# Separate places for the q copies of two head pairs, and a written TensorE order at the start

## The chip, the cores and the metric

The kernel runs on one core of one Trainium2 chip. The metric is the device time of one execution in microseconds; the figure is the median over several runs. Times on a trace are microseconds from the start of the span.

## The reference

The reference chains three stages over 8 sequences of 576 tokens and 512 features (8 heads of 64).

```
scores = (q @ k^T) / sqrt(64), masked in blocks of 64 (row block >= column block)
attn   = exp(scores - max); attn /= sum + 1e-9;  x = attn @ v          # attention
gate   = sigmoid(causal convolution of x with 5 taps per feature)
x      = (gate * (x @ w_val)) @ w_out                                  # gated convolution
u      = x + real(fft over tokens and features of x)                   # Fourier mixing
un     = (u - mean) / sqrt(var + 1e-6)
out    = u + relu(un @ w_ch1) @ w_ch2                                  # feed-forward layer
```

All of it is float32. The kernel holds it by splitting each operand of a matmul into a high part and a low rest (hi + lo) and adding two or three products.

## The kernel before, in words

The program has two phases. `phase2` is the feed-forward layer; it is not touched. `phase1` does attention, gated convolution and Fourier mixing, batch by batch. The change lies in its first part.

Attention goes by head pairs: two heads of one sequence share the 128 partitions, 64 rows each. There are 32 pairs, four to a sequence, and each is cut into nine units (NB = 9): units 0 to 7 are the four query blocks of 128 rows for either head, unit 8 holds the last 64 rows of both heads. The main loop (L973) runs over units n = 9 * p + i and issues, for each n, work of several ages: the score matmuls of unit n (`emit_qk`), row maxima (`emit_max`) and exponentials (`emit_exp`) of a unit or two before, the transposes of the probabilities of unit n - 6 (`emit_t`), and, at two places of the first five pairs, the product with v (`emit_near`). Behind every fourth pair a dense stage for that sequence (`dense`: psv, psx, psy and pss matmuls) is appended and taken in small steps beside later units. How many steps a unit takes is set by a credit: RATE0 = 0.9 a unit up to n = N0 = 60, RATE = 1.25 after it. The preparation of weights (`prep_weights`: loads into XA, decoding on ScalarE and VectorE, folds on POOL, then the DFT tables into `dft_t`) moves along with the steps.

Before its scores, q and k of a pair are loaded by SP (`load`, L346 and L348) into two raw buffers, and `split` makes high and low parts: `k_hi` (L57 by `copy`), `k_dup` (four SP copies, L385), `k_lo` (POOL, L380), `q_hi` (ScalarE, L366) and `q_lo` (VectorE, L369) into QHL, and `q_last` (two SP copies into QD, L374), which feeds unit 8. `spread(p, g)` then sends QHL on to the tiles QQ[h][g] that the score matmuls read (L427, L428): for either head one SP copy of the high part (L398) and one of the low part (L400), so four for each half g. Half g = 0 feeds units 0 to 3, half g = 1 units 4 to 7. QHL and QQ exist once. So q of pair p + 1 may be split only when the copies of pair p have gone out, and a half of QQ may be overwritten only when the score matmuls of pair p that read it are done: split(p + 1) is issued in unit 0 of pair p, its two halves are spread in units 4 and 8.

The stages of `split` form a `Chain`: `tick` runs one stage of each open chain, twice in a unit.

A planner orders the instructions of each engine ahead of time: of those whose inputs it believes ready, the one that was issued first in the program goes first. An engine then runs in that fixed order, and waits on semaphores where an input is late.

Of the kernel before, what the change touches and what calls it, by code (L numbers as in the profile page):

```python
# [17 lines left out]
def kernel(  # L18
# [14 lines left out]
    B, NP, P, S = q.shape  # L33
# [73 lines left out]
    def k_places():  # L107
        return [kp.tile([P, S], F32R, tag=t, name=t) for t in ("K0", "K1", "KP", "KL")]
# [4 lines left out]
    def w_places(f, t):  # L113
        WQ[f] = [x[:, 0:D] for x in t]
# [12 lines left out]
    def phase1():  # L127
        with ExitStack() as c1:
# [14 lines left out]
            QHL = pa.tile([P, 2, S], F32R, name="QHL")  # L143

            QD = [pa.tile([P, 2, P], F32R, name=f"QD{i}") for i in range(2)]

            QQ = [[pa.tile([P, 2, 256], F32R, name=f"QQ{h}{g}") for g in range(2)] for h in range(2)]
# [18 lines left out]
            GH = [pool.tile([P, 2 * N2], F32R, name=f"GH{c}") for c in range(4)]  # L166
# [6 lines left out]
            dft_t = pool.tile([P, dft.shape[1]], F32R, name="dft")  # L173
# [162 lines left out]

            NPAIR = B * NP
            qraw, kraw, KK, KP, KL, VV = {}, {}, {}, {}, {}, {}
            rs = [slice(0, 64), slice(64, 128)]

            def load(p):
# [16 lines left out]
            def split(p):  # L358
                if p >= NPAIR:
                    return  # L360

                *KK[p], KP[p], KL[p] = k_places()
                kk, kh, kl = KK[p], KP[p], KL[p]

                def q_hi():
                    nc.scalar.activation(out=QHL[:, 0, :], in_=qraw[p], func=AF.Copy, scale=0.125)  # L366

                def q_lo():
                    nc.vector.scalar_tensor_tensor(out=QHL[:, 1, :], in0=qraw[p], scalar=0.125,  # L369
                                                   in1=QHL[:, 0, :].bitcast(F32), op0=ALU.mult, op1=ALU.subtract)  # L370

                def q_last():
                    for r in rs:
                        nc.sync.dma_start(out=QD[p % 2][r, :, r].bitcast(F32), in_=QHL[r, :, D:S].bitcast(F32))  # L374

                def k_hi():
                    copy(0, kh, kraw[p])

                def k_lo():
                    nc.gpsimd.tensor_tensor(out=kl, in0=kraw[p], in1=kh.bitcast(F32), op=ALU.subtract)  # L380

                def k_dup():
                    for h in range(2):
                        for r in rs:
                            nc.sync.dma_start(out=kk[h][r, :].bitcast(F32), in_=kh[rs[h], :].bitcast(F32))  # L385

                def both(*f):
                    return lambda: [g() for g in f]

                return Chain(k_hi, both(k_dup, k_lo), wait, q_hi, q_lo, q_last)  # L390

            def spread(p, g):

                if p >= NPAIR:
                    return
                c = slice(256 * g, 256 * g + 256)
                for h in range(2):
                    nc.sync.dma_start(out=QQ[h][g][rs[h], :, :].bitcast(F32),  # L398
                                      in_=QHL[rs[h], 0:1, c].bitcast(F32).to_broadcast([64, 2, 256]))
                    nc.sync.dma_start(out=QQ[h][g][rs[1 - h], 0, :].bitcast(F32), in_=QHL[rs[h], 1, c].bitcast(F32))  # L400
# [12 lines left out]
            def emit_qk(n):  # L413
                p, i = divmod(n, NB)
                if i in (1, 3):

                    return
                if i < 8:

                    L = P * (i // 2 + 1)  # L420
                    w = max(256, L)
                    m = slice(P * (i // 2 % 2), P * (i // 2 % 2) + P)
                    t = sc_tile(n)
                    for u in range(2 if i < 4 else 1):
                        h, o = (u, w * u) if i < 4 else (i % 2, 0)
                        q = QQ[h][i // 4]
                        nc.tensor.matmul(t[:, o:o + w], q[:, 0, m], KK[p][h][:, 0:w], start=True, stop=False)  # L427
                        nc.tensor.matmul(t[:, o:o + w], q[:, 1, m], KL[p][:, 0:w], start=False, stop=True)  # L428
                        scs[n + u] = [(t[:, o:o + L], 0, L)]
                    if i < 4:  # L430
                        twos[n] = t.rearrange("p (h w) -> p h w", h=2)[:, :, 0:L]
                    return

                sc = []
                for k0, w in ((0, 320), (320, 256)):
                    t = sc_tile(n)
                    mm3(t[:, 0:w], QD[p % 2][:, 0], QD[p % 2][:, 1], KP[p][:, k0:k0 + w], KL[p][:, k0:k0 + w], True, True)
                    sc.append((t[:, 0:w], k0, w))
                scs[n] = sc
# [470 lines left out]
            NU = NPAIR * NB  # L910
            LT = 6
# [8 lines left out]
            LA = 1  # L920
# [2 lines left out]
            PN = 5  # L923
            EW = 4
            EX = 3
            N0 = 60
            RATE0 = 0.9
            RATE = 1.25
            N1 = 30
# [11 lines left out]
            prepared = [0]  # L941
            load(0)
            nc.gpsimd.memset(PB[8][:, S:640], 0.0)
            for t in QD + [QQ[h][g][rs[1 - h], 1, :] for h in range(2) for g in range(2)]:
                nc.gpsimd.memset(t.bitcast(F32), 0.0)
            split(0).run()
            spread(0, 0)
            spread(0, 1)
            load_v(0)
            load(1)  # L950
            pend = [prep]
# [1 line left out]
            credit = 0.0  # L953
# [16 lines left out]
                        pend.pop(0)  # L970

            now[0] = 1
            for n in range(NU + LT + LA):  # L973
                if n == N1:
                    now[0] = 0
                p, i = divmod(n, NB)
                credit += RATE if n > N0 else RATE0
                nst = int(credit)
                credit -= nst
                if n < NU:  # L980
                    if i == 6:
                        load(p + 2)
                    if i == 7:
                        load_v(p + 1)
                    if i == 0:
                        split(p + 1)
                    emit_qk(n)
                    if i in (4, 8):
                        spread(p + 1, i // 8)
                    if p == NPAIR - 1 and i in (0, EW):  # L990
                        if i == 0:
                            w_places(0, k_places())
                        for z in range(2):
                            first_weights(2 * (i > 0) + z)
                if n in (NU, NU + EX):

                    if n == NU:
                        w_places(1, k_places())
                    for z in range(2):
                        first_weights(4 + 2 * (n > NU) + z)  # L1000
                old = list(live)
                step(nst // 2)
                tick(old)
                advance(0, n, emit_max, 1)
                advance(1, n, emit_exp)
                pr, ir = divmod(n - FR, NB)
                if n >= FR and PN <= pr < NPAIR and ir == 0:
                    emit_recip(pr)
                old = list(live)
                if 0 <= n - LT < NU:  # L1010
                    emit_t(n - LT)
                advance(0, n, emit_max)
                m = n - LT - LA
                if 0 <= m < NU:
                    pm, im = divmod(m, NB)
                    if pm < PN:
                        if im in (2, 7):
                            emit_recip_near(pm, im // 7)
                        if im == 3:
                            emit_near(pm, 0)  # L1020

                    if im == 8:

                        while pm % NP == 0 and gate_done[0] < pm // NP:
                            step()
                        if pm % NP == 0 and pm:
                            folds[4 * (pm // NP) - 2].run(2)
                        while pm % NP == 1 and pm > NP and val_done[0] < pm // NP:
                            step()
                        if pm < PN:  # L1030
                            emit_near(pm, 1)
                        else:
                            emit_av(pm)
                        if pm % NP == NP - 1:
                            pend.append(dense(pm // NP))
                step(nst - nst // 2)
                tick(old)
                if n >= FR and PN <= pr < NPAIR and ir == 1:
                    emit_factors(pr)
            while pend:  # L1040
                if not drain[0]:
                    drain[0] = 3
                old = list(live)
                step()
                tick(old)
# [611 lines left out]
```

## Time and profile before

| | us |
|---|---|
| median of 3 runs | 1408.18 (1406.77 to 1408.38) |
| the profiled execution, its own time | 1406.78 |
| its span on the trace | 1405.0 |
| TensorE busy in the span | 1349.6 (96%) |
| VectorE (DVE) busy | 1094.1 (78%) |
| ScalarE (ACT) busy | 821.1 (58%) |

Busy times of an engine are the union of its instructions; a busy TensorE is not TensorE at its peak, since the matmuls are pipelined and the granted clock can be lower. An engine's idle time costs nothing where another engine is the bottleneck. Engines in the rows: PE is TensorE, PEld its weight loads, DVE VectorE, ACT ScalarE, POOL GpSimd, SP SyncE, which issues nearly all DMAs (SPq is its queue).

### The profile page before, as it was taken

The numbers are of one execution on the slowest core, as the hardware profiler recorded it, in microseconds if no ns is written. First come the engines' busy times: TensorE is split into PE (matmuls) and PEld (weight loads), VectorE is DVE, ScalarE is ACT, GpSimd is POOL, SyncE is SP. The second block draws the span as 40 slices with busy tenths as digits, with TensorE's granted clock in tenths as the row PEclk, the third lists the DMA queues.
The fourth block names the chain that finished last, engine by engine and source line by source line (L and its number), as shares of the span: only waits on it lengthen the run. The fifth ranks groups of instructions, "written<-read, shape, count | busy, mean of one in ns | idle before, by whom it ended". The sixth has DMA issues, their size and how long they took to land.

```text
span 1405.0 us, 24014 instructions
## 1 busy us (share of the span) xinstructions
PE 1349.6 (96%) x8547; PEld 1186.2 (84%) x8547; DVE 1094.1 (78%) x1965; ACT 821.1 (58%) x1790; POOL 207.7 (15%) x180
## 2 busy tenths in 40 slices
PE   5798999999999999999999999999999999999998
PEld 3576799898989998888777887788888889999998
DVE  5867787887878797989899798599746983796274
ACT  5687777777777777764344244574356534744451
POOL 2423232323232232322100000000000000000000
PEclk9799999999999999999999999999999999999999
DMA  7566566656556565646598996985875479779875
GB/s 211 138 176 189 158 182 154 186 139 176 153 158 158 153 164 155 173 149 236 198 369 290 356 316 211 319 273 195 280 266 201 180 248 328 256 250 319 273 250 188
DMA packets 176755, 308.24 MB, mean 219 GB/s; under 512 B 28270, under 2 KB 106876, under 8 KB 169468
## 3 DMA queue, kind: packets, MB, share of 16 engines
q1 hardware_dynamic: 176096, 306.57, 69.2%
q8 instruction: 68, 1.11, 0.3%
q14 instruction: 51, 0.42, 0.1%
q10 hardware_dynamic: 540, 0.14, 0.1%
HBM read 203.74 MB, written 56.76 MB: 185 GB/s over the span
## 4 chain that ended last, share of the span: by engine, by line
PE 73%; DVE 12%; DMA 5%; ACT 3%; issue 3%; POOL 2%; SPq 2%; DVEq 0%; ACTq 0%; POOLq 0%
PE banks L1421 12%; PE banks L1423 12%; PE banks L1422 12%; PE av L615 4%; PE pt L587 4%; DVE gate L642 2%; PE sc L427 2%; PE o L1518 2%; PE psh L1498 2%; PE psh L1496 2%; PE psh L1497 2%; PE o L1516 2%; PE o L1517 2%; PE sc L428 2%; POOL XA L848 1%
## 5 line engine op out<-in xcount | busy, mean ns | idle before, releaser
L1421 PE MATMUL banks<-o,chunk 128*128 128x512 f32 (+1 forms) x896 | 324.2, 362 | 1.0 <-ACT h L1429 1.0
L1422 PE MATMUL banks<-o,chunk 128*128 128x512 f32 (+1 forms) x896 | 323.9, 362 | 0.0
L1423 PE MATMUL banks<-o,chunk 128*128 128x512 f32 (+1 forms) x896 | 323.9, 362 | 0.0
L473 ACT ACTIVATE PB<-sc,mx 128x128 f32<-128x128 f32 (+4 forms) x320 | 166.5, 525 | 51.0 <-DVE mx L459 27.8
L1421 PEld LDWEIGHTS banks<-o,chunk 128*128 128x128 f32 x896 | 168.2, 188 | 19.1 <-ACT h L1429 1.7
L1423 PEld LDWEIGHTS banks<-o,chunk 128*128 128x128 f32 x896 | 168.2, 188 | 17.6
L1422 PEld LDWEIGHTS banks<-o,chunk 128*128 128x128 f32 x896 | 168.2, 188 | 17.2
L1381 ACT CAST o<-h 128x1024 fp32r<-128x1024 f32 (+1 forms) x112 | 105.4, 944 | 106.9 <-PE banks L1423 86.5
L587 PE MATMUL pt<-ident,PB 128*128 128x128 f32 x800 | 141.9, 283 | 15.1 <-ACT PTb L593 8.2
L1382 DVE TENSOR_TENSOR o<-h,o 128x1024 fp32r<-128x1024 f32 (+1 forms) x112 | 119.7, 1083 | 23.3 <-ACT o L1381 22.9
L587 PEld LDWEIGHTS pt<-ident,PB 128*128 128x128 f32 x800 | 101.0, 144 | 31.9 <-ACT PTb L593 14.5
L642 DVE SCALAR_TENSOR_TENSOR gate<-XF,cw,gate 128x575 f32<-128x575 f32 (+3 forms) x128 | 122.5, 957 | 4.3 <-ACT gate L63 3.6
L459 DVE TENSOR_REDUCE mx<-sc 128x1 f32<-128x384 f32 (+2 forms) x192 | 104.2, 560 | 4.4 <-PE sc L193 2.7
L427 PE MATMUL sc<-K,QQ 128*128 128x256 f32 (+2 forms) x256 | 87.7, 353 | 13.5 <-DMA QQ<-QHL 12.6
L593 ACT COPY PTb<-pt 128x512 f32<-128x512 f32 (+1 forms) x160 | 86.5, 544 | 18.5 <-PE pt L587 17.6
L1429 ACT COPY h<-banks 128x1024 f32<-128x1024 f32 (+1 forms) x64 | 58.0, 906 | 57.3 <-PE banks L1423 57.3
L191 PE MATMUL psx<-GH,we_h 128*128 128x290 f32 x256 | 83.5, 326 | 2.4 <-ACT GH L57 1.5
L191 PE MATMUL psv<-XH,wv_h 128*128 128x288 f32 x256 | 83.5, 327 | 0.4 <-ACT PB L473 0.4
L428 PE MATMUL sc<-KL,QQ 128*128 128x256 f32 (+2 forms) x256 | 82.8, 334 | 0.0
L638 POOL TENSOR_TENSOR XL<-XF,XH 128x576 fp32r<-128x576 f32 x32 | 45.9, 1433 | 249.6 <-ACT XH L57 228.8
L192 PE MATMUL psx<-GL,we_h 128*128 128x290 f32 x256 | 76.2, 298 | 0.5 <-DVE GL L703 0.5
L192 PE MATMUL psv<-XL,wv_h 128*128 128x288 f32 x256 | 76.2, 298 | 0.0
(266 smaller groups left out, 3151.3 us busy)
## 6 DMA issues: line engine op xcount, KB each, us to landing
chunk<-comb_d SPq DMA_DIRECT2D x64, 512.0 KB, 5.0
chunk<-comb_d SPq DMA_DIRECT2D x32, 1024.0 KB, 4.8
chunk<-base_d SPq DMA_DIRECT2D x48, 512.0 KB, 5.9
chunk<-base_d SPq DMA_DIRECT2D x24, 1024.0 KB, 6.3
K<-KP SPq DMA_DIRECT2D x128, 144.0 KB, 2.5
QQ<-QHL SPq DMA_DIRECT2D x128, 128.0 KB, 2.4
rw<-in_w_ch SPq DMA_DIRECT2D x28, 512.0 KB, 8.3
comb_d<-packed SPq DMA_DIRECT2D x12, 1024.0 KB, 10.1
```

The lines of the kernel that those rows point to most:

```text
L191: nc.tensor.matmul(ps, lh, rh, start=first, stop=False)
L192: nc.tensor.matmul(ps, lh, rl, start=False, stop=False)
L427: nc.tensor.matmul(t[:, o:o + w], q[:, 0, m], KK[p][h][:, 0:w], start=True, stop=False)
L428: nc.tensor.matmul(t[:, o:o + w], q[:, 1, m], KL[p][:, 0:w], start=False, stop=True)
L473: nc.scalar.activation(out=PB[i][:, k0:k0 + w], in_=t, func=AF.Exp, bias=nm, accum_out=su[:, at + j:at + j + 1])
L587: nc.tensor.transpose(ps[:, j, :], PB[i][:, (j0 + j) * P:(j0 + j + 1) * P], ident)
L642: nc.vector.scalar_tensor_tensor(out=gate[c][:, s:S], in0=XF[:, 0:S - s], scalar=cw[:, c, 4 - s:5 - s], in1=gate[c][:, s:S], op0=ALU.mult, ...
L1381: nc.scalar.copy(out=o[:, 0], in_=x)
L1382: nc.vector.tensor_tensor(out=o[:, 1], in0=x, in1=o[:, 0].bitcast(F32), op=ALU.subtract)
L1421: nc.tensor.matmul(to, wh, o[:, 0, x], start=first, stop=False, skip_group_check=not begin)
L1422: nc.tensor.matmul(to, wh, o[:, 1, x], start=False, stop=False, skip_group_check=not begin)
L1423: nc.tensor.matmul(to, wl, o[:, 0, x], start=False, stop=last, skip_group_check=not begin)
```

## The change

Pairs 1 and 3 (odd, and up to EARLY = 3) get q copies in other places, `QQ2` and `QHL2`. These are views of tiles that are used only later: QQ2 of GH (the dense stage's operand), QHL2 of `dft_t` (the DFT tables). For pairs 0 to 4, `split` issues the eight spreading copies directly behind `q_lo` and ahead of `q_last`, without the empty stage, in place of units 4 and 8 of the pair before. The zeros that QQ needs in its unused half are written for QQ2 too. The rate of the dense steps rises at N0 = 50 in place of 60. And the body of the unit loop becomes a function, which for n < 40 runs under a schedule in which TensorE's instructions keep the order in which the program issues them.

```diff
+            EARLY = 3
+            QQ2 = [[GH[2 * h + g][:, 0:512].rearrange("p (z c) -> p z c", z=2) for g in range(2)] for h in range(2)]
+            QHL2 = dft_t[:, 0:2 * S].rearrange("p (z s) -> p z s", z=2)
+
+            def q_places(p):
+                return (QQ2, QHL2) if p % 2 and p <= EARLY else (QQ, QHL)
...
+                QHL = q_places(p)[1]
...
+                if p <= EARLY + 1:
+                    return Chain(k_hi, both(k_dup, k_lo), q_hi, q_lo, lambda: spread(p, 0), lambda: spread(p, 1), q_last)
                 return Chain(k_hi, both(k_dup, k_lo), wait, q_hi, q_lo, q_last)
...
+                QQ, QHL = q_places(p)
...
-                        q = QQ[h][i // 4]
+                        q = q_places(p)[0][h][i // 4]
...
-            N0 = 60
+            N0 = 50
...
-            for t in QD + [QQ[h][g][rs[1 - h], 1, :] for h in range(2) for g in range(2)]:
+            for t in QD + [x[h][g][rs[1 - h], 1, :] for x in (QQ, QQ2) for h in range(2) for g in range(2)]:
                 nc.gpsimd.memset(t.bitcast(F32), 0.0)
             split(0).run()
-            spread(0, 0)
-            spread(0, 1)
...
-            for n in range(NU + LT + LA):
+            def unit(n):
+                nonlocal credit
...
-                    if i in (4, 8):
+                    if p > EARLY and i in (4, 8):
                         spread(p + 1, i // 8)
...
+            for n in range(NU + LT + LA):
+                if n < 40:
+                    with tc.manual_schedule(engines=set([mybir.EngineType.PE])):
+                        unit(n)
+                else:
+                    unit(n)
```

## Rows read from the trace of the kernel before

**Rows 1.** The first page: busy time by engine, and the chain that ended last.

```profile
PE 1349.6 (96%) x8547; PEld 1186.2 (84%) x8547; DVE 1094.1 (78%) x1965; ACT 821.1 (58%) x1790; POOL 207.7 (15%) x180
...
PE 73%; DVE 12%; DMA 5%; ACT 3%; issue 3%; POOL 2%; SPq 2%; DVEq 0%; ACTq 0%; POOLq 0%
```

**Rows 2.** Busy by stage: stretch, length, PE, PEld, DVE, ACT, POOL, PEclk, DMA share, GB/s.

```profile
0.00:80.00 80.00, 53.69 (x270) 37.41 (x271) 52.54 (x129) 47.92 (x135) 29.59 (x46) 0.85 0.64 173
80.00:160.00 80.00, 72.19 (x527) 58.41 (x526) 59.58 (x147) 62.75 (x179) 25.01 (x25) 0.98 0.67 179
160.00:320.00 160.00, 156.76 (x1342) 142.46 (x1341) 131.37 (x308) 121.12 (x357) 47.19 (x34) 1.00 0.62 164
```

**Rows 3.** The same table, cut at the first score matmul of pairs 0 to 7.

```profile
11.72:30.38 18.66, 15.45 (x60) 10.45 (x60) 9.44 (x30) 10.99 (x34) 5.16 (x6) 0.82 0.74 206
30.38:50.21 19.83, 14.55 (x76) 10.48 (x76) 15.99 (x35) 11.62 (x32) 6.15 (x5) 0.77 0.58 158
50.21:70.46 20.25, 14.93 (x84) 10.29 (x82) 16.74 (x36) 14.05 (x41) 11.06 (x14) 0.84 0.54 147
70.46:84.68 14.22, 12.99 (x89) 9.74 (x88) 9.62 (x29) 11.84 (x36) 3.52 (x4) 0.95 0.54 138
84.68:99.82 15.14, 15.09 (x100) 10.35 (x99) 9.32 (x28) 12.36 (x37) 4.18 (x4) 1.00 0.73 190
99.82:118.91 19.09, 17.11 (x130) 15.03 (x128) 16.00 (x45) 14.24 (x40) 6.80 (x8) 1.00 0.67 173
118.91:143.40 24.49, 20.12 (x147) 16.02 (x146) 18.14 (x44) 19.05 (x53) 5.79 (x6) 0.93 0.78 226
```

**Rows 4.** TensorE in order of time: start, length, line, operation, [idle before it].

```profile
21.16 0.69 PE L587 MATMUL pt<-ident,PB 128*128 128x128 f32 x2 [1.89 <-ACT PTa L593]
...
30.38 0.39 PE L427 MATMUL sc<-K,QQ 128*128 128x256 f32 x1
...
38.65 0.69 PE L427 MATMUL sc<-K,QQ 128*128 128x384 f32 x1
```

**Rows 5.** SP's issues and one ScalarE row in order of time, 0 to 25 us.

```profile
8.16 1.28 SPq L374 DMA_DIRECT2D QD<-QHL  x2
...
9.49 0.60 SPq L400 DMA_DIRECT2D QQ<-QHL  x1
...
17.35 0.69 ACT L366 ACTIVATE QHL<-qraw 128x576 fp32r<-128x576 f32 x1 [0.78 <-DMA qraw<-in_q]
...
19.45 2.49 SPq L385 DMA_DIRECT2D K<-KP  x4
...
23.35 1.24 SPq L400 DMA_DIRECT2D QQ<-QHL  x2
```

**Rows 6.** TensorE's waits, 0 to 330 us: total, times, longest.

```profile
PE sc L427 <- DMA QQ<-QHL: 12.6, 2, 11.7
```

**Rows 7.** The chain that ended last, in order of time, 0 to 140 us.

```profile
14.00 3.11 DMA qraw<-in_q
...
29.90 4.02 DMA QQ<-QHL
...
70.74 2.52 DMA QQ<-QHL
...
98.62 8.52 DMA XA<-in_w_out
```

**Rows 8.** POOL: QQ's memsets (ns min/median/max, first and last start), and its first subtraction.

```profile
L945 POOL MEMSET QQ<- x4: 304/305/306, 1.9 to 2.8; 64x256 f32 x4
...
5.25 1.40 POOL L380 TENSOR_TENSOR KL<-kraw,KP 128x576 fp32r<-128x576 f32 x1 [2.17 <-ACT KP L57]
```

**Rows 9.** One 4 us stretch with its granted clock, columns as in rows 2.

```profile
48.00:52.00 4.00, 3.41 (x16) 3.06 (x16) 3.41 (x8) 3.50 (x11) 0.18 (x1) 0.50 0.87 253
```

**Rows 10.** Two successive matmuls of the dense stage on TensorE.

```profile
147.54 0.30 PE L193 MATMUL psx<-GH,we_l 128*128 128x290 f32 x1
147.68 0.30 PE L191 MATMUL psx<-GH,we_h 128*128 128x290 f32 x1
```

## The prediction

> **What bounds the kernel now.** I read four views, from coarse to fine. The first page says that TensorE is busy 1349.6 us of a span of 1405.0 and holds 73% of the chain that ended last [rows 1]. So time comes back in two ways only: fewer idle stretches of TensorE, or work that stands earlier behind an idle stretch. The table by stage tells where the idle time is [rows 2]: the first 80 us hold 53.69 us of TensorE work (26.3 idle), the next 80 us 72.19 (7.8 idle), and the next 160 us 156.76, which is full. DVE and ACT are 82% and 76% busy in that full stage, so they keep up there. What a change at the front saves, the full stages behind it can therefore pass on one for one to the end.
>
> The third view cuts the front at the first score matmul of each head pair: pair 0 at 11.72, then 30.38, 50.21, 70.46, 84.68 and 99.82 [rows 3]; the row of one of these matmuls, pair 1's, stands in [rows 4], the other five look like it. The first three pairs take 18.66, 19.83 and 20.25 us, the fourth and fifth 14.22 and 15.14. TensorE was busy 14.55 us or more of the three long ones only because its granted clock was 0.77 to 0.84 in them; in one 4 us stretch it was 0.50, the 1.2 GHz level, with 3.41 us busy [rows 9]. Pair 3 carries the same attention work in 12.99 us at 0.95. In pairs 1 and 2 DVE has the most work for its length, 15.99 and 16.74 us, since the decoding of the first weights runs there.
>
> The last view says what the long pairs wait for. TensorE's own wait for q copies, after the start, is one of 0.9 us (12.6 in total, 11.7 of it the first) [rows 6]. That looks as if the copies did not matter. The chain says otherwise: it passes through the landing of a QQ copy issued at 29.90 (4.02 us) and of another at 70.74 (2.52 us) [rows 7]. The wait is hidden because the order of TensorE was planned around it: the first scores of pair 1 run at 30.38, behind all transposes of pair 0, and its scores of unit 4 only at 38.65, eight microseconds later [rows 4].
>
> **The change part by part.** Working is against the profiled execution (1406.78 us, which is the span and 1.78 around it); the median shown is 1.40 above it, and I add that at the end.
>
> *The start.* SP issues the four K copies, then two QD copies (8.16), then the first low q copy (9.49), on which the first matmul at 11.72 waits. The QD copies move behind the eight QQ copies, so that one goes out at 8.16: 1.33 us earlier. QD is needed only by unit 8 and has eight issues of about 0.65 us to land behind. The later issues do not move: the load of pair 1 still stands behind the same fourteen copies, at 14.00 [rows 5, 7]. So this saves between 0 and 1.33 us at pair 0, and nothing at pair 1; I carry nothing. The four new memsets on POOL, 0.305 us each, 1.2 in all, fall in the 2.17 us in which POOL sat idle before its first subtraction [rows 8]: nothing. Without that cover they would delay KL by up to 1.2 us.
>
> *Pair 1.* Its q arrives at 17.3 and is split from 17.35 on in both kernels. Before, SP sends four K copies from 19.45 to 21.94, QD, and only at 23.35 the two low copies of the first half; the second half is sent around loads, the last of it at 29.90, because a place is reused and because it is traced at units 4 and 8 of pair 0 [rows 5, 7]. After, places are free and everything is traced in units 1 to 3: the two low copies follow the K copies at 21.9 and 22.5, and with about 2.5 us to landing (the 70.74 copy took 2.52) the first scores can run at 25.2, not 30.38: 5.2 us. The second half needs four more issues, 2.6 us, and lands at about 27.7, far ahead of 38.65. Both ends: nothing, if ACT and DVE are late with q, and 6 us, if SP sends the low copies ahead of K. I take 5.2. Queued behind this on SP is the load of pair 2: with two QD copies ahead of it, it goes at about 26.5, and with the 3.1 us of pair 1's load (14.00 to 17.1 in the chain [rows 7]) its data is there by 30.
>
> *TensorE's order.* Units 0 to 39 run as written: scores of unit n, then transposes of unit n-6, then the near product. The transposes of unit 3 of pair 0, which ran at 21.16 [rows 4], now stand behind the first scores of pair 1 and wait until 25.2: 4.0 us of ready work held up. In return scores of unit 4 on no longer stand behind a whole pair's transposes, so DVE and ACT have maxima and exponentials to do while TensorE transposes. I price the holding at 2 us over the four pairs (ends: 0, and 4.0 in each of four pairs).
>
> *Pairs 1 to 3.* With q and K copied nine units ahead, what is left in pairs 1 and 2 is work. The fullest engine is DVE with 15.99 and 16.74 us; TensorE at the clock it had needs 14.55 and 14.93 [rows 3]. I take DVE's work and a twentieth more, 17.0 and 17.5: savings of 2.8 and 2.7 us. The ends are 0 (as long as before) and 14.22 each, the length of pair 3, if the decoding moves into pair 3 (5.6 and 6.0). Pair 3 keeps its 14.2: nothing. Pair 4 uses the old places again, but they were last read by pair 2, so it is ready early too; its 15.14 us hold 15.09 of TensorE: nothing.
>
> So the first scores of pair 4 come at 25.2 + 17.0 + 17.5 + 14.2 = 73.9 instead of 84.68, 10.8 earlier; less 2 for the holding, 8.8.
>
> A rule of the Trainium skill speaks against the order: in "TensorE: Matmul & The Clock Gate", section "Part 2: What happens when you issue a matmul", matmuls stay in program order and only weight loads are pulled ahead, so a matmul that waits holds all that stand behind it. The trace shows the same, and its price here is the 4.0 us above; by that rule alone the sum goes to the slower rival below.
>
> *The faster rate from unit 51.* Ten units at 1.25 instead of 0.9 bring 3.5 steps of the dense work forward. Successive psx matmuls start 0.14 us apart (147.54 and 147.68) [rows 10] and a step has six: 0.84 us, so 2.9 us of TensorE work leave the end. These units lie near 112 to 132 us, where TensorE idles 2.0 of 19.09 and 4.4 of 24.49 us [rows 3], but DVE and ACT are 74 to 84% busy there. Between a loss of 2.9 and a gain of 2.9 I take a gain of 0.4.
>
> *Sum.* 8.8 + 0.4 = 9.2 us off 1406.78 gives 1397.6 in the profiled execution, and off the median of 1408.18 gives 1399.0.
>
> **The rivals.**
> First, only the first handover gains. DVE's decoding fills pairs 1 and 2 to the length they had, and what remains is 5.2 less 2 for holding: 1408.2 - 3.2 = 1405.0. For it: DVE is the fullest engine of both. Against: it was only 81 and 83% busy over them [rows 3], and the decoded weights have no reader before the dense steps, which the code begins behind pair 3.
>
> Second, nothing arrives at the end. Pairs 5 and 6 wait for the weights decoded from w_out and the DFT tables, and pair 6 takes 24.49 us in which no engine is full [rows 3]; if that stretch is as long as its transfers and not as its units, it gives the 9 us back: 1408. For it: the chain lies for 8.52 us in a load of w_out there [rows 7]. Against: those loads are issued by unit, so they move forward with the pairs, and DMA has room (0.64 of its share in the first 80 us [rows 2]).
>
> Third, slower: the written order holds TensorE. Each first score of pairs 1 to 4 waits for its K and q copies while ready transposes stand behind it, 4.0 us each as at pair 1, ACT gets its transposes later, and the gaps keep the clock at the lower level as in [rows 9]. Then four times 4.0 less the 5.2 at pair 1 is 10.8 more: 1419.0. It decides once pair 4's first scores come after 87.5 us (84.68 and 2.8). Against: each later pair has nine units, some 15 us, between its split and its first scores, and the raw buffers it needs are free after the split.
>
> A fourth, larger gain: decoding moves into pair 3 and clock stays up, pairs 1 and 2 take 14.22 each, and 5.2 + 5.6 + 6.0 + 1.3 + 0.4 = 18.5 less 2 gives 1391.7.
>
> **How the numbers follow.** The forecast with 6 to 13 us gained has 0.50, its own range 1395 to 1402. The first rival has 0.18, the second 0.13, the third 0.13, the fourth 0.06. A difference of 0.2%, 2.8 us, is about what a measurement of this kernel tells from no change. Faster beyond it: 0.50 + 0.18 + 0.06 = 0.74; within: 0.13; slower: 0.13. The range runs from 1391, below which only the far end of the fourth lies, to 1409, which takes in the first and the second and leaves out the third.
>
> **What would show it.** Right: first scores of pairs 1 to 4 near 25, 42, 60 and 75; the first 80 us with some 60 us of TensorE work instead of 53.7; SP with the eight QQ copies of pair 1 in one row; stages from 160 us on as full as before. Wrong in the first step if pair 1 starts at 28 or later; in the DVE step if pairs 1 and 2 still take 19 us or more with DVE not full; in the passing on if pair 4 is early and pair 8 is not; in the order step if TensorE shows new waits above 2 us in front of scores in its first 40 units.

## The result and the profile after

The changed kernel takes 1417.54 us (1412.2 to 1422.03) against 1407.57 us of the kernel before beside it: a ratio of 1.0072, 95% interval 1.0051 to 1.0093. It is slower by some 10 us, where a gain of 9.2 us was forecast. The profiled execution took 1416.4 us with a span of 1414.6.

The first page of the changed kernel, which answers to [rows 1]:

```profile
PE 1349.0 (95%) x8547; PEld 1187.7 (84%) x8547; DVE 1110.4 (78%) x1965; ACT 823.7 (58%) x1790; POOL 213.1 (15%) x184
...
PE 54%; DVE 6%; ACT 2%; DMA 1%; issue 1%; SPq 0%; POOL 0%; DVEq 0%; ACTq 0%; POOLq 0%
```

TensorE does the same 8547 matmuls in nearly the same busy time, so the 9.6 us that the span grew show as idle time of TensorE. The second line can't be set against that of [rows 1]: the shares add up to 64%, since this chain could be followed back only to 493.8 us. Where is the time lost? The stage windows of the changed kernel, columns as in [rows 2], here with the stretch after them:

```profile
0.00:80.00 80.00, 51.94 (x311) 40.41 (x313) 59.64 (x147) 53.24 (x151) 34.16 (x52) 0.87 0.71 191
80.00:160.00 80.00, 72.54 (x555) 60.35 (x551) 62.53 (x147) 64.08 (x183) 26.10 (x26) 1.00 0.67 183
160.00:320.00 160.00, 152.68 (x1285) 138.23 (x1286) 129.37 (x292) 116.51 (x337) 47.24 (x32) 0.99 0.59 155
...
320.00:480.00 160.00, 155.29 (x1341) 139.90 (x1340) 127.92 (x297) 117.99 (x341) 45.78 (x33) 1.00 0.58 156
```

and that last stretch in the kernel before:

```profile
320.00:480.00 160.00, 158.01 (x1381) 144.09 (x1380) 128.06 (x306) 119.97 (x352) 47.07 (x34) 1.00 0.61 161
```

Read the counts, not the busy time, in the first two rows: TensorE did 311 and 555 matmuls where it did 270 and 527, so the front is ahead, though its busy time in the first 80 us fell. The third row turns round, 1285 matmuls instead of 1342, and so does the last, 1341 instead of 1381.

The same is seen by following one operation that each pair has once, the first copy of its k on ScalarE. For pairs 8, 12, 19 and 31 of the changed kernel:

```profile
138.88 0.66 ACT L57 CAST KP<-kraw 128x576 fp32r<-128x576 f32 x1
...
210.46 0.68 ACT L57 CAST KP<-kraw 128x576 fp32r<-128x576 f32 x1
...
349.30 0.67 ACT L57 CAST KP<-kraw 128x576 fp32r<-128x576 f32 x1
...
580.71 0.67 ACT L57 CAST KP<-kraw 128x576 fp32r<-128x576 f32 x1
```

and of the kernel before:

```profile
148.91 0.67 ACT L57 CAST KP<-kraw 128x576 fp32r<-128x576 f32 x1
...
218.72 0.68 ACT L57 CAST KP<-kraw 128x576 fp32r<-128x576 f32 x1
...
349.70 0.68 ACT L57 CAST KP<-kraw 128x576 fp32r<-128x576 f32 x1
...
573.74 0.68 ACT L57 CAST KP<-kraw 128x576 fp32r<-128x576 f32 x1
```

So the changed kernel is 10.0 us ahead at pair 8, 8.3 at pair 12, level at pair 19, and 7.0 behind at pair 31. By 139 us it has won a little more than the forecast; then it loses 17 us in stages whose work the change does not touch, and 2.6 us more behind pair 31.

The front itself, cut at the first score matmul of pairs 0 to 5 (columns as in [rows 3]):

```profile
11.00:24.22 13.22, 6.66 (x26) 5.82 (x27) 10.07 (x30) 8.32 (x27) 4.53 (x6) 0.84 0.78 225
24.22:39.82 15.60, 13.98 (x83) 10.31 (x84) 11.66 (x31) 10.37 (x33) 5.22 (x5) 0.80 0.71 194
39.82:56.85 17.03, 12.53 (x84) 9.51 (x84) 14.45 (x36) 14.00 (x40) 8.66 (x10) 0.90 0.70 192
56.85:77.61 20.76, 16.39 (x101) 12.89 (x102) 16.15 (x39) 15.82 (x46) 9.78 (x10) 0.84 0.65 165
77.61:93.58 15.97, 13.32 (x94) 9.50 (x93) 13.44 (x31) 13.46 (x39) 7.06 (x9) 1.00 0.63 166
```

Pair 1 starts at 24.22 and pair 4 at 77.61 instead of 84.68.

TensorE's waits from 200 to 640 us, by the line that waited and what came last (total, times, longest), in the changed kernel. The same statements have other line numbers than in the kernel before (scores L438 for L427, transposes L598 for L587). `re` are the reciprocals of the softmax sums, `rt` their transposes, `pt` the transposes of the probabilities, PTa and PTb where ScalarE puts them; psv, psx, psy and pss are steps of the dense stage.

```profile
PE rt L507 <- DVE re L497: 8.7, 7, 2.4
PE pt L598 <- ACT PTb L604: 1.4, 2, 1.0
PE pt L598 <- ACT PTa L604: 1.2, 2, 0.8
PE psv L191 <- DVE XA L883: 1.2, 4, 0.3
PE psv L191 <- DVE gv L691: 0.7, 3, 0.2
```

and the two longest in the kernel before:

```profile
PE rt L496 <- DVE re L486: 2.9, 8, 0.6
PE pt L587 <- ACT PTb L593: 2.7, 5, 0.6
```

There no wait stands in front of psv. Each of these waits is short, but they come back.

### The profile page after: what moved, and what is told of

It reads as the page before. It is cut to its first block, busy times and chain, and to the rows that moved or that the text cites. A ratio compares the mean times of both kernels' runs of the same rounds, so it can differ in the third digit from the quotient of the medians.

```text
span 1414.6 us, 23984 instructions
## 1 busy us (share of the span) xinstructions
PE 1349.0 (95%) x8547; PEld 1187.7 (84%) x8547; DVE 1110.4 (78%) x1965; ACT 823.7 (58%) x1790; POOL 213.1 (15%) x184
## 4 chain that ended last, share of the span: by engine, by line
PE 54%; DVE 6%; ACT 2%; DMA 1%; issue 1%; SPq 0%; POOL 0%; DVEq 0%; ACTq 0%; POOLq 0%
PE banks L1438 12%; PE banks L1439 12%; PE banks L1440 12%; PE o L1535 2%; PE psh L1515 2%; PE psh L1513 2%; PE psh L1514 2%; PE o L1533 2%; PE o L1534 2%; PE av L626 1%; PE pt L598 1%; DMA rw<-in_w_ch 1%; PE psx L192 1%; PE psx L193 1%; PE psx L191 1%
## 5 line engine op out<-in xcount | busy, mean ns | idle before, releaser
L598 PE MATMUL pt<-ident,PB 128*128 128x128 f32 x800 | 139.9, 280 | 6.1 <-ACT PTb L604 4.3
L653 DVE SCALAR_TENSOR_TENSOR gate<-XF,cw,gate 128x575 f32<-128x575 f32 (+3 forms) x128 | 136.3, 1065 | 5.9 <-ACT gate L63 5.0
L598 PEld LDWEIGHTS pt<-ident,PB 128*128 128x128 f32 x800 | 100.9, 144 | 17.7 <-ACT PTb L604 9.8
L438 PE MATMUL sc<-K,QQ 128*128 128x256 f32 (+1 forms) x240 | 81.7, 351 | 18.3 <-DMA QQ<-QHL 13.9
L439 PE MATMUL sc<-KL,QQ 128*128 128x256 f32 (+1 forms) x240 | 77.8, 335 | 0.0
```

Of the source, the lines that this page charges most:

```text
L598: nc.tensor.transpose(ps[:, j, :], PB[i][:, (j0 + j) * P:(j0 + j + 1) * P], ident)
L653: nc.vector.scalar_tensor_tensor(out=gate[c][:, s:S], in0=XF[:, 0:S - s], scalar=cw[:, c, 4 - s:5 - s], in1=gate[c][:, s:S], op0=ALU.mult, ...
```

## The experiments

Two edits of the change act on these later stages: the rate from N0 = 50, and the written order, whose end sets what the planner begins with. Theory A is the rate, theory B the new plan as such.

**The rate put back in the changed kernel.**

```diff
-            N0 = 50
+            N0 = 60
```

> The changed kernel with N0 back at 60. The comparison of the two traces shows the changed kernel 8 to 10 us ahead up to pair 11 and then losing it pair by pair, to 9.5 us behind at the end of attention. Theory A, the rate: the 3.5 dense steps that N0 = 50 brings forward make every dense stage run nearer to its inputs, and each sequence loses some 2.5 us. Then this kernel keeps what the front gained: 8 to 10 us less than the kernel before, 1398 to 1400, ratio 0.993 to 0.994. Theory B, the new plan: whatever changes the front re-plans the order of all engines behind it, and the steady part is slower whatever the rate: 1413 to 1420, ratio 1.004 to 1.009.

Measured 1402.78 us, ratio 0.9966 (0.9953 to 0.9979): faster than the kernel before. The k copies of pairs 8, 12, 19 and 31 are at

```profile
143.22 0.67 ACT L57 CAST KP<-kraw 128x576 fp32r<-128x576 f32 x1
...
214.78 0.68 ACT L57 CAST KP<-kraw 128x576 fp32r<-128x576 f32 x1
...
346.50 0.68 ACT L57 CAST KP<-kraw 128x576 fp32r<-128x576 f32 x1
...
569.48 0.68 ACT L57 CAST KP<-kraw 128x576 fp32r<-128x576 f32 x1
```

which is 5.7, 3.9, 3.2 and 4.3 us ahead of the kernel before: most of what the front wins stays won. Theory B is out, and theory A has the sign, but the gain is 4.2 us where it expected 8 to 10.

**The rate alone, in the kernel before.**

```diff
-            N0 = 60
+            N0 = 50
```

> The kernel before with N0 = 50 alone. Theory A, the rate: the front is as before, the steady part loses as in the changed kernel, some 17 us from pair 9 to the end of attention: 1420 to 1426, ratio 1.009 to 1.013. Theory B, the new plan: the rate matters for ten units only, 1405 to 1410, ratio 0.998 to 1.002.

Measured 1431.53 us, ratio 1.0169 (1.0155 to 1.0183). One number in a front that nothing else changes costs 24.5 us, more than theory A expected.

**The changed kernel with all of TensorE's order planned.**

```diff
-                if n < 40:
+                if n < 0:
```

> The changed kernel with TensorE's order left to the planner in all units (N0 = 50 stays). Theory A, the rate: the steady loss stays, and the front tells what the written order was worth: first scores of pair 4 near 77.6 if it was worth nothing, later if it helped; total 1412 to 1424. Theory B, the new plan: another plan, another steady part; anything from 1398 to 1420. What was forecast (holding costs 2 us) would make the front 2 us earlier.

Measured 1428.91 us, ratio 1.0159 (1.0142 to 1.0176), above the range of either theory; pair 4 starts at 84.21, near the 84.68 of the kernel before. So the early start of pair 4 needs the written order.

**The written order alone, in the kernel before** (the loop's body as a function `unit`, as in the change).

```diff
+                if n < 40:
+                    with tc.manual_schedule(engines=set([mybir.EngineType.PE])):
+                        unit(n)
```

> The kernel before with the written TensorE order in its first 40 units and nothing else. The q copies of pair 1 still land at about 27 and 33, so the written order has to wait for them: first scores of pair 4 at 88 to 92 instead of 84.7. Theory A, the rate: N0 is 60, so the steady part is that of the kernel before and the loss of 3 to 7 us is kept: 1411 to 1415. Theory B, the new plan: another steady part, up to 1425.

Measured 1402.35 us, ratio 0.9972 (0.9963 to 0.9981). The expectation had the sign wrong: the order alone is worth 4.7 us, as much as order and copies together. Its first scores of pair 1, with q copies in the one old place, on TensorE in order of time (last column: idle before, and what ended it):

```profile
25.02 0.55 PE L427 MATMUL sc<-K,QQ 128*128 128x256 f32 x1 [5.50 <-DMA QQ<-QHL]
```

and pair 4's run at 77.35:

```profile
77.35 0.36 PE L427 MATMUL sc<-K,QQ 128*128 128x256 f32 x1
```

**Lead or phase.** The rate reaches the dense steps through a running sum: each unit adds 0.9 or 1.25 and takes as many whole steps as the sum has gained. An earlier start does two things. The sum is 3.5 steps ahead at unit 60 (45.9 + 10 x 1.25 = 58.4 against 54.9). This lead shrinks by one in each group of 36 units, since the rate gives 45 steps to a dense stage of 46 and a loop (L1028 of the kernel before) takes the missing one by force, until it is gone at unit 168 (in pair 18, about 360 us). And the remainder of the sum is 0.4 instead of 0.9, which decides which of every four units takes two steps: with 54.9 + 1.25 the sum passes two whole numbers at unit 61, so n mod 4 = 1; with 45.9 + 1.25 at unit 51, so n mod 4 = 3. As 36 is a multiple of 4, that stays so to the end. The traces show both: ahead of the first scores of pairs 9, 13, 17, 19 and 22, TensorE has started 269, 530, 791, 914 and 1124 dense matmuls in the changed kernel, and 245, 517, 786, 915 and 1130 in the kernel before (six make a step of psv or psx). Theory L is the lead, theory P the phase. Between the k copies of pairs 19 and 31, where hardly any lead is left, the changed kernel still loses 7.4 us, which speaks for P; four kernels tell it.

Lead without the phase (N0 = 50, half a step taken off):

```diff
+                if n == 51:
+                    credit -= 0.5
```

> The changed kernel with half a step taken off the sum of the rate at unit 51. The second rate starting at unit 51 does two things: up to unit 160 the steps of the dense queue stand 3, then 2, then 1 earlier (lead), and of every four units a different one takes two steps, the one with n mod 4 = 3 instead of n mod 4 = 1, in every group of 36 units to the end (phase). Here the lead stays and the phase is again that of the kernel before. Theory P (the phase costs it): 1401 to 1405 us, as with the rate at unit 60 (1402.8). Theory L (the lead costs it, and what is lost while the queue is ahead stays lost): 1413 to 1419 us, as the changed kernel (1417.5).

Phase without the lead (N0 = 60, half a step added):

```diff
+                if n == 61:
+                    credit += 0.5
```

> The changed kernel with the second rate at unit 61 again, and half a step added to the sum at unit 61: no lead to speak of, but the phase of the changed kernel (two steps in the units with n mod 4 = 3). Theory P: 1412 to 1419 us, and the loss against the kernel with the rate at unit 60 grows by 2 to 3.5 us in each group of 36 units up to the end of the attention. Theory L: 1401 to 1405 us.

The other two phases, the same with 0.25 and with 0.75:

```diff
-                    credit += 0.5
+                    credit += 0.25
```

> The changed kernel with the second rate at unit 61 again, and a quarter of a step added to the sum there: two steps in the units with n mod 4 = 0. Theory P: a time of its own, 1399 to 1420 us, away from 1402.8 by over 2 us on either side. Theory L: 1401 to 1405 us.

```diff
-                    credit += 0.5
+                    credit += 0.75
```

> The changed kernel with the second rate at unit 61 again, and three quarters of a step added to the sum there: two steps in the units with n mod 4 = 2. Theory P: a time of its own, 1399 to 1420 us, away from 1402.8 by over 2 us on either side. Theory L: 1401 to 1405 us.

All six on the front of the changed kernel:

| two steps where n mod 4 is | lead at unit 60 | us | ratio to before (95%) |
|---|---|---|---|
| 1 (rate from 61) | 0 | 1402.78 | 0.9966 (0.9953 to 0.9979) |
| 1 | 3 | 1406.81 | 1.0003 (0.9992 to 1.0013) |
| 2 | 0 | 1413.33 | 1.0049 (1.0035 to 1.0064) |
| 0 | 0 | 1416.07 | 1.0064 (1.0049 to 1.0079) |
| 3 | 0 | 1419.42 | 1.0089 (1.0075 to 1.0103) |
| 3 (the change) | 3.5 | 1417.54 | 1.0072 (1.0051 to 1.0093) |

Theory P holds: each of the four phases has its own time, and the phase of the change alone costs 16.6 us (1419.42, just above the 1412 to 1419 expected). The lead alone costs 4.0, outside what theory P expected (1401 to 1405), so L has a small part; together the two give 14.8, less than their sum. (The kernel before measured 1406.6 to 1407.6 beside them, so these differences hold within a microsecond or so.) With all of TensorE's order planned the same edit costs more, 24.5 us above and 22.1 with the copies. Why it is more was not tried, but the traces show where (below).

In the full stretch the loss is steady. From the first exponential of pair 16 to that of pair 28 (three groups of four pairs), against the kernel with the rate at 61, the phase alone loses 3.0, 2.8 and 3.0 us, the changed kernel 2.5, 2.8 and 2.7, the lead alone 0.7, 0.0 and -0.1.

Windows of the full stretch, with the rate at 61, then the phase alone (two kernels):

```profile
320.00:480.00 160.00, 158.00 (x1383) 144.23 (x1383) 129.41 (x310) 120.12 (x352) 47.40 (x34) 1.00 0.60 161
```

```profile
320.00:480.00 160.00, 155.41 (x1339) 139.35 (x1338) 128.34 (x295) 117.31 (x341) 44.38 (x33) 1.00 0.58 155
```

The granted clock is 1.00 in both, and no other engine has become the bound: all do less. Busy time fell by 1.6%, matmuls by 3.2%; the last section shows how far busy time can be trusted here. TensorE's waits from 200 to 640 us, with the rate at 61, the phase alone, and phase 0:

```profile
PE rt L507 <- DVE re L497: 3.0, 8, 0.8
PE pt L598 <- ACT PTb L604: 2.7, 5, 0.6
```

```profile
PE rt L507 <- DVE re L497: 7.2, 7, 1.3
PE psv L191 <- DVE XA L883: 1.6, 5, 0.3
PE pt L598 <- ACT PTa L604: 1.4, 2, 0.9
PE psv L191 <- DVE gv L691: 1.2, 5, 0.2
PE pss L191 <- DVE XA L843: 0.9, 5, 0.2
```

```profile
PE sc L438 <- ACT PB L484: 4.2, 11, 0.5
PE rt L507 <- DVE re L497: 2.7, 8, 1.1
```

To see the whole of it, I add up, between the exponentials that begin pairs 12 and 28 (four sequences), the distance from each matmul's start to the next one's, under the tile that the later one writes (2539 to 2550 records each; ave, 10.1 to 10.4 in all, is left out). The last two rows have the phase of the first. In us:

```
                    all     pt    psx   sc    psv   av    pss   psy   rt
rate from 61        297.6   53.1  50.7  50.5  50.3  37.5  19.9  19.2   6.4
phase 3 alone       309.3   51.8  50.9  52.0  55.4  37.3  23.0  19.4   9.4
phase 2             308.0   53.5  51.1  54.1  51.6  38.8  19.6  19.9   8.8
phase 0             304.3   51.2  50.8  57.0  51.3  37.4  20.6  20.6   5.4
the changed kernel  310.5   53.1  50.2  52.6  54.3  38.3  21.5  19.2  11.0
the lead alone      299.7   53.1  50.6  50.9  50.9  37.6  20.1  18.9   7.4
the kernel before   298.0   53.1  51.2  51.1  50.3  37.5  19.9  19.3   5.6
```

In phase 3 it is psv, pss and the transposes of the reciprocals (rt) that start later behind their forerunners; in phase 0 the scores; in phase 2 the scores and rt, and less so psv and av. No one wait is the culprit in all. That each phase puts other steps just ahead of their inputs, in an order that is fixed ahead, is my reading of these rows; why n mod 4 = 1 meets the fewest late inputs stays open.

The same stretch, pair 12 to pair 28, takes 309.3 to 310.5 us in all four kernels whose doubled step falls where n mod 4 = 3, with a written or a planned front, and 297.2 to 299.7 in all seven where it is 1. So the planned order loses no more there. The rate alone in the kernel before loses its 24.5 us (25.4 between the profiled executions) as 6.4 ahead of pair 12, 12.5 in this stretch and 6.6 behind pair 28; the changed kernel, against the rate at 61, gains 2.8 in the first part and loses 12.9 and 1.9 in the others (12.0 between the profiled executions). In phase 0 the part behind pair 28, 7.1 us, is as large as the 6.7 in the stretch; what happens behind pair 28 was not followed up.

**The copies alone** (the changed kernel with the rate from 61 and all of TensorE's order planned).

```diff
-            N0 = 50
+            N0 = 60
...
-                if n < 40:
+                if n < 0:
```

> The second places for the q copies and their early issue alone: the changed kernel with TensorE's order planned in all units, as before, and the second rate from unit 61. Theory O (the written order carries the gain of the front, the copies none): 1405 to 1408.5 us, pair 1's first scores near 29 and pair 4's near 84 us, as in the kernel before. Theory C (the copies are worth something by themselves, and the written order only its part): 1401 to 1404.5 us, pair 4's first scores at 78 to 82 us.

Measured 1406.85 us, ratio 1.0006 (0.9997 to 1.0015). Theory O holds: in their free places and issued early, the copies change nothing without the written order (pair 4's first scores run at 85.69). Pair 1's first scores still stand behind the products of pair 0:

```profile
30.73 0.43 PE L565 MATMUL av<-PTb,VV 128*64 128x320 f32 x1
31.09 0.38 PE L438 MATMUL sc<-K,GH 128*128 128x256 f32 x1
```

with no wait ahead of them; they are late by plan. (GH in such a row is QQ2, and dft QHL2: the profile gives the names of the tiles that they are views of.)

**How much of the written order is needed**, in the kernel before: 18 units, and 72.

```diff
-                if n < 40:
+                if n < 18:
```

> The kernel before with TensorE's order written only in the first 18 units (pairs 0 and 1). If the gain is made at the first handover (pair 1 at 25.0 instead of 30.4 us) and only carried on: pair 4 at 77 to 80 us and 1401 to 1404 us. If the written order has to hold in each of the four pairs: pair 4 at 81 to 85 us and 1404.5 to 1408 us.

```diff
-                if n < 40:
+                if n < 72:
```

> The kernel before with TensorE's order written in the first 72 units (pairs 0 to 7), into the stretch where TensorE is nearly full. If the written order is better wherever inputs come late, 1397 to 1402 us. If it is worth only as much as the first handovers, 1401 to 1404 us. If the planned order is the better one in the full stretch, where transposes and dense work can fill a wait, 1404 to 1415 us.

With 18 units 1401.98 us, ratio 0.9970 (0.9959 to 0.9982), and pair 4 at 78.48, both as expected if the gain is made at pairs 0 and 1 and carried on. The k copies of pairs 12 and 19 of this kernel,

```profile
212.67 0.68 ACT L57 CAST KP<-kraw 128x576 fp32r<-128x576 f32 x1
...
343.64 0.68 ACT L57 CAST KP<-kraw 128x576 fp32r<-128x576 f32 x1
```

are both 6.1 us ahead of the kernel before: these full stages pass a gain on whole, if the phase stays. With 72 units 1403.61 us, ratio 0.9984 (0.9972 to 0.9995), inside the second expectation (1401 to 1404): no better than the first handovers. The versions with 18 and with 40 written units, and the change with the rate at 61, beat both kernels and can't be told from each other.

## Why the prediction was wrong

**The faster rate from unit 51** is the step that failed. It counted 3.5 steps of 0.84 us, with a loss of 2.9 or a gain of 2.9 as its ends, and took a gain of 0.4. Its reasoning was about the lead alone, and the lead alone costs 4.0 us, outside both ends; 3.0 of them are lost by pair 12 (its k copy runs at 217.79 against 214.78). The changed kernel is 4.3 us ahead of the kernel with the rate at 61 at pairs 8 and 12, but 1.9 of that is there at pair 4 already (77.61 against 79.48), before unit 50, and with the lead alone none of it is seen, so it can't be put down to the lead. What the step left out is the remainder of the sum. That moved the doubled step to other units in every later group of 36, at 2.5 to 3.0 us each once steady, and the two together cost 14.8 us, five times the far end of the step. Less the 4.2 us that the front brings, this makes the 10 us of the result. The number to look at stood in the code: 0.9 x 51 and 0.9 x 61 leave different fractions.

**Passing on one for one** holds roughly where the phase is kept, and not here. With 18 written units, 6.1 us at pair 12 are 6.1 us at pair 19, though 4.2 at the end. The forecast took "full" to mean that only the work counts; the stage of 156.76 us in 160 [rows 2] holds 152.68 after, with the same work to do in another order.

**TensorE's order** was priced as a loss of 2 us and is the source of the whole gain of the front, 4.2 to 4.7 us at the end. The first scores of pair 1 in the changed kernel hold up what stands behind them,

```profile
24.22 0.55 PE L438 MATMUL sc<-K,GH 128*128 128x256 f32 x1 [6.56 <-DMA GH<-dft]
```

an idle stretch of 6.56 us. The fifth transpose of pair 0, which ran at 21.16 [rows 4], stands behind these scores and runs at 25.89, 4.7 us later, where 4.0 were expected:

```profile
25.89 1.27 PE L598 MATMUL pt<-ident,PB 128*128 128x128 f32 x5
```

The Trainium skill ("TensorE: Matmul & The Clock Gate", section "Part 2: What happens when you issue a matmul") says that matmuls stay in program order; the trace agrees by this transpose. But the time went the other way (1402.35 us with the order alone). The forecast counted mainly what is held up. The planned order of the kernel before put the scores of pair 1 behind all of pair 0's transposes [rows 4], and DVE was busy only 9.44 of 18.66 us in the stretch ahead of them [rows 3]; asking for the scores first costs a wait and gives DVE and ACT pair 1's work 5 us earlier. With the order alone ACT does 52.05 us of work in the first 80, DVE 54.79 and TensorE 295 matmuls, where [rows 2] has 47.92, 52.54 and 270. That the order is the source is shown by the runs; that it gains in this way is argued from these rows.

**Pair 1** came at 24.22, near the forecast 25.2, but not for its reason. The free places do not bring it (31.09 with the copies alone), and the old places suffice (25.02 with the order alone), as the copies for the first scores went out early enough before too (the low ones at 23.35 [rows 5]). SP does what was forecast, eight copies in one row from 21.19 to 25.78:

```profile
18.73 2.41 SPq L393 DMA_DIRECT2D K<-KP  x4
21.19 0.62 SPq L409 DMA_DIRECT2D GH<-dft  x1
...
25.78 0.60 SPq L411 DMA_DIRECT2D GH<-dft  x1
```

The chain through the copies of 29.90 and 70.74 [rows 7] was read as a price of the places, but with free places and the planned order nothing was gained.

**Pairs 1 to 3** were forecast at 17.0, 17.5 and 14.2 us and took 15.60, 17.03 and 20.76. DVE's work over the three was 42.4 us before (15.99 + 16.74 + 9.62 in [rows 3]) and 42.3 after (11.66 + 14.45 + 16.15), but it moved from pair 1 into pair 3. What moved in is not the decoding, as in the fourth rival: its DVE lines (L75 to L82) took 6.4, 4.5 and 0.0 us in the three pairs before and 3.2, 4.2 and 0.5 after. It is the taps of the convolution's gate (L642, now L653): 2.3, 3.7 and 2.7 us before, 0.0, 4.3 and 7.0 after. So pair 4 came 7.1 us earlier, not 8.8. No engine is full in pair 3 (TensorE is busy 16.39 of 20.76 us, DVE 16.15); what bounds it was not tried.

**The rivals.** The third had the sign, and its 1419.0 is near the measured time by luck: its mechanism would have put pair 4 after 87.5, and it came at 77.61. None of the four looked at the stages behind pair 6, and no row read for the forecast bears on which unit takes which step.

**The signs named ahead.** The first 80 us were to hold some 60 us of TensorE work and hold 51.94, with 41 matmuls more than before: busy time did not count the work here. The stages from 160 us on were to be as full as before and were not (152.68 us of 160 for 156.76): this sign told against the forecast, and rightly. The passing-on test (pair 4 early, pair 8 not) was set too near: pair 8 was early, and the loss came behind it. The sign against the order, a new wait above 2 us in front of scores, was there (6.56 us), and pointed the wrong way: the order is what gained.

## What to carry to other kernels

Where work is handed out by a running sum, a change of its start or rate also changes the remainder, and if the loop's length is a multiple of the pattern, that shift is repeated to the end: price it per loop, or hold the remainder fixed. A stage in which TensorE is busy 98% of the time (156.76 of 160 us here) can lose several microseconds to order alone, so follow one operation per pair through both traces before crediting or blaming the stretch that was edited. And before freeing a buffer, see whether the reader waits for it or merely stands behind other work in a fixed order.

## What the runs showed of the hardware

Short waits between pipelined matmuls are only partly visible as idle time. Between the exponentials that begin pairs 12 and 28 the phase alone takes 11.7 us longer than the kernel with the rate at 61 for the same work (309.3 against 297.6). TensorE's idle time grows by only 4.5 of them (4.8 to 9.3 us), and 7.2 count as busy (292.8 to 300.0), at a granted clock of 1.00 from 320 to 480 us in both. Counts in equal windows, or distances from start to start, show the whole loss.
